# Reordering A's q and k weight columns on chip, so that most head rows skip the DRAM scratch

## The chip, the cores and the metric

One core of a Trainium2 chip runs the kernel. The time is device microseconds of one execution; the number given for a kernel is the median of several runs. TensorE (PE in the profile) multiplies, VectorE (DVE) and ScalarE (ACT) read its results out of PSUM, GpSimd (POOL) masks, and SyncE (SP) issues nearly all DMAs.

## The reference

Two attention blocks on inputs of 2048 tokens and 640 features, 32 heads of 20 features each; their outputs lie side by side. Block A is softmax attention within a sliding window of 256 tokens, block B is linear attention:

```python
def _A_ref(x, wqkv, wo):
    H = 32; Dh = D // H; W = 256
    q, k, v = qkv[0], qkv[1], qkv[2]            # (x @ wqkv) by heads
    scores = jnp.einsum("bhqd,bhkd->bhqk", q, k) * (Dh ** -0.5)
    mask = (idx[:, None] - idx[None, :] >= 0) & (idx[:, None] - idx[None, :] < W)
    p = _softmax(jnp.where(mask, scores, -1e9), axis=-1)
    o = jnp.einsum("bhqk,bhkd->bhqd", p, v)
    return o.reshape(B, S, D) @ wo

def _B_ref(x, wqkv, wo):
    phi = lambda t: jnp.where(t > 0, t + 1, jnp.exp(t)) + 1e-6
    pq, pk = phi(q), phi(k)
    kv = jnp.einsum("bhsd,bhse->bhde", pk, v);  z = jnp.einsum("bhsd->bhd", pk)
    num = jnp.einsum("bhqd,bhde->bhqe", pq, kv)
    den = jnp.einsum("bhqd,bhd->bhq", pq, z)[..., None] + 1e-6
    return (num / den).reshape(B, S, D) @ wo
```

## The kernel before

Tokens are worked in four super-blocks `s` of 512. The heads of A are taken in eight groups of four. For the scores, TensorE runs the four heads of a group side by side in four strips of 32 rows, so q and k are wanted in "pads": tiles of 128 partitions by 8 groups by 512 tokens in which head j of a group lies on partitions 32j to 32j+19. The projection gives its rows packed, 20 to a head, so before the change every q and k row takes a trip through DRAM: `a_rows(n, s)` computes five chains of five 128x512 matmuls (L208), casts each to a stage tile `st` (L198), writes it to a scratch tensor, and `bounce` queues four reads (L277) that put the rows into the pad. For s = 0 the writes are issued on ACT's queue chunk by chunk (L309), for the others as one transfer on SP (L273); the reads are issued by `drip` within later work, or by `drop` at once.

The main loop takes 90 score tiles (18 for s = 0, then 24 each). `scores` puts up to four blocks of 128 x 128 of each of four heads into `S_ps`, which fills half of PSUM and has one buffer (L587). ACT takes the exponential of all 2048 columns into `p` (L595), after a one-element copy into `p` that takes the waits for that buffer (L580), and POOL masks the edges (L609). Two tiles later `values` multiplies by v (16 matmuls of 21 columns, L631) into `O_ps`, one buffer too, and after the last tile of a head group VectorE divides by the row sums (recA L653, otokA L654). The first tile of s = 0 (form "X") takes the diagonal block of groups 0 to 3, and the tile with that of groups 4 to 7 comes at index 9.

All the other work is a generator `fill`, from which `take` draws matmuls between tiles: q, k and v of A's later super-blocks, B's projections and `b_kv`, `b_q`, `b_den`, `b_merge`, output projections. Its unit is columns of TensorE work. `credit` gives each tile an equal share of it:

```python
    take(EARLY)
    units = [u for s in range(NS) for u in tiles_of(s)]
    LAG = 2
    rate = (FILL - TAIL - LAG * NO_VALUES) / len(units)
```

`EARLY` is 25600 columns, which are the q and k rows of s = 1: they are computed ahead of tile 0, while the pads of s = 0 come back from DRAM. `TAIL` columns stay for after the last tile. Fill matmuls go to one of three PSUM banks `dense`, which VectorE (or ACT near the end) has to read before PE takes the bank again. `phi` is computed by an ACT exponential `e` (L218) and two VectorE steps (L221, L224), of which the latter are put off (`later`, `flush`). `b_den` flushes them and makes the reciprocal denominators rden (L535, L536), and `quotients` multiplies by them on VectorE (L547), with DMA transposes before and after on SP's queue.

The order of instructions on each engine is the program's order. The kernel starts with loads of x and of A's v, q and k weights on SP's queue in this order, then x of s = 1 (a DMA transpose) and B's k weights. PE runs a few dummy matmuls, transposes x, computes v of s = 0 (`a_v(0)`, casts to vA on VectorE), then q and k of s = 0, the early fill, and tile 0.

Of the kernel before, what the change touches and what calls it, by code (L numbers as in the profile page):

```python
# [9 lines left out]
P = 128  # L10
ALU = mybir.AluOpType
ACT = mybir.ActivationFunctionType
ENG = mybir.EngineType
BF16 = mybir.dt.bfloat16
# [3 lines left out]
DH = 20  # L18
HV = DH + 1
NG = H // 4  # L20
SB = 512
TPS = SB // P

EARLY = 25600
FILL = 357760
TAIL = 17920

NO_VALUES = 1024
# [26 lines left out]
def kernel(  # L55
# [10 lines left out]
    nc = tc.nc  # L66
    _, S, D = A_x.shape
    KT = D // P
# [8 lines left out]
    def pool(name, bufs, space=None):  # L77
        if space is None:
            return ctx.enter_context(tc.tile_pool(name=name, bufs=bufs))
        return ctx.enter_context(tc.tile_pool(name=name, bufs=bufs, space=space))  # L80

    wp = pool("weights", 1)
    xp = pool("x", 2)
    qp = pool("q", 2)
    kp = pool("k", 3)
    vp = pool("v", 3)
    pp = pool("p", 3)
    stp = pool("stage", 2)
    bp = pool("b", 1)
    pqp = pool("pq", 2)  # L90
    op1 = pool("o1", 2)
# [10 lines left out]
    w_sb = {}  # L102
    wo_sb = {}
    for n in "AB":
        w_sb[n] = wp.tile([P, KT, 3 * D], BF16, name=f"w{n}")
        wo_sb[n] = wp.tile([P, KT + (n == "B"), D], BF16, name=f"wo{n}")

    def load_w(n, src, i, eng, lo=0, hi=D):
        wv = src.rearrange("(kt p) n -> p kt n", p=P)
        cols = slice(i * D + lo, i * D + hi)  # L110
        eng.dma_start(out=w_sb[n][:, :, cols], in_=wv[:, :, cols])

    xsrc = {"A": A_x[0], "B": B_x[0]}

# [68 lines left out]
    def flush(before=None):  # L183

        while later and (before is None or later[0][0] <= before):
            later.pop(0)[1]()
# [3 lines left out]
    def evac(dst, src, to=None):  # L190

        if to is None and both:
            both.append(to)
            to = "AD"[len(both) % 2]
        if to == "A":
            nc.scalar.activation(out=dst, in_=src, func=ACT.Copy)
        else:
            nc.vector.tensor_copy(out=dst, in_=src)  # L198

    def bank():  # L200
        flush(begun[0] - 2)
        begun[0] += 1
        return dps.tile([P, SB], F32, name="dense")

    def chain(dst, lhs, rhs, n):

        for kt in range(KT):
            nc.tensor.matmul(  # L208
                dst, lhsT=lhs(kt), rhs=rhs(kt), start=(kt == 0), stop=(kt == KT - 1)
            )  # L210
            if kt < KT - 1:
                yield n
# [22 lines left out]
    def banks(g, n):  # L235

        for _ in range(n):
            for c in g:
                yield c
                if isinstance(c, End):  # L240
                    break
# [22 lines left out]
    xA, xB = {}, {}  # L264
    q_pad, k_pad, v_tok = {}, {}, {}

    reads = {}

    def bounce(n, s, scratch, st, dst):


        if s > 0:
            nc.sync.dma_start(out=scratch.rearrange("(c p) n -> p c n", p=P), in_=st[:])  # L273
        sv = scratch.rearrange("(g j d) n -> j d g n", j=4, d=DH)

        def read(j):
            nc.sync.dma_start(out=dst[32 * j : 32 * j + DH, :, :], in_=sv[j])  # L277

        reads[n, s] = [(read, j) for j in range(4)]

# [12 lines left out]
            fn(j)  # L293

    def a_rows(n, s):
        base = 0 if n == "q" else D
        st = stp.tile([P, KT, SB], BF16, name="st")
        scratch = tc.dram_tile([D, SB], BF16, name=f"{n}_scr{s}")
        for c in range(KT):
            ps = bank()  # L300
            yield from chain(
                ps[:],
                lambda kt: w_sb["A"][:, kt, base + c * P : base + (c + 1) * P],
                lambda kt: xA[s][:, kt, :],
                SB,
            )
            evac(st[:, c, :], ps[:])
            if s == 0:
                nc.scalar.dma_start(out=scratch[c * P : (c + 1) * P, :], in_=st[:, c, :])  # L309
            if c == KT - 1:  # L310
                pad, pl, name = (q_pad, qp, "qpad") if n == "q" else (k_pad, kp, "kpad")
                pad[s] = pl.tile([P, NG, SB], BF16, name=name)
                bounce(n, s, scratch, st, pad[s])
            yield End(SB)

    def a_qk(s, between=()):
# [5 lines left out]
    def hook(gen, n, fn):  # L322

        for i, c in enumerate(gen):
            if i == n:
                fn()
            yield c

    hh = H // 2
    by_tokens = [(tb, i) for tb in range(TPS) for i in range(2)]  # L330

    def v_proj(n, xt, dst, order=by_tokens):
        for tb, i in order:
            ps = bank()
            yield from chain(
                ps[:, 0 : hh * DH],
                lambda kt: xt[:, kt, tb * P : (tb + 1) * P],
                lambda kt: w_sb[n][:, kt, 2 * D + i * hh * DH : 2 * D + (i + 1) * hh * DH],
                hh * DH,
            )  # L340
            evac(
                dst[:, tb, i * hh : (i + 1) * hh, 0:DH],
                ps[:, 0 : hh * DH].rearrange("p (h d) -> p h d", d=DH),
            )
            yield End(hh * DH)
# [7 lines left out]
    def a_v(s):  # L353
        v_tok[s] = v_bufs[s % 3]
        order = by_tokens
        if s == 0:
            order = [(0, 0), (1, 0), (0, 1), (1, 1), (2, 0), (2, 1), (3, 0), (3, 1)]
        yield from v_proj("A", xA[s], v_tok[s], order)
# [50 lines left out]
    def b_kv(s):  # L409
        pk = pqp.tile([P, TPS, D], BF16, name="phi")  # L410

        def done(tb, ps):
            if tb is None:
                phi(pk[:, :, SB:D], ps, lambda t: t[:].rearrange("p (t n) -> p t n", n=P))
            else:
                phi(pk[:, tb, 0:SB], ps[:])

        rows = tok_rows(xB[s], w_sb["B"], D, done)
        values_of = v_proj("B", xB[s], vB)
        yield from even(rows, TPS + 1, values_of, TPS + 1)  # L420
        yield from values_of
        flush()
        for cs in (range(0, 3), range(3, KT)):
            ps = bank()
            pv = ps[:, 0 : len(cs) * NHC * HV].rearrange("p (c h e) -> p c h e", h=NHC, e=HV)
            for i, c in enumerate(cs):
                for tb in range(TPS):
                    nc.tensor.matmul(  # L428
                        pv[:, i, :, :],
                        lhsT=pk[:, tb, c * P : (c + 1) * P],  # L430
                        rhs=vB[:, tb, GH * c : GH * c + NHC, :],
                        start=(tb == 0),
                        stop=(tb == TPS - 1),
                    )
                if c != cs[-1]:
                    yield TPS * P + P
            at = slice(cs[0], cs[-1] + 1)
            acc = kv_acc[:, at, :, :]
            if s == 0:
                nc.vector.tensor_copy(out=acc, in_=pv)  # L440
            elif s < NS - 1:
                nc.vector.tensor_tensor(out=acc, in0=pv, in1=acc, op=ALU.add)
            else:
                for dst, h0, h1, e0, e1 in (
                    (zk, 0, NHC, DH, HV), (six, 0, GH, 0, DH), (two, GH, NHC, 0, DH)
                ):
                    nc.vector.tensor_tensor(
                        out=dst[:, at, :, :],
                        in0=pv[:, :, h0:h1, e0:e1],
                        in1=acc[:, :, h0:h1, e0:e1],  # L450
                        op=ALU.add,
                    )
            yield TPS * P + P
# [235 lines left out]
    def run(gen):  # L689
        for _ in gen:  # L690
            pass
# [22 lines left out]
    def load(n, s):  # L714
        if n == "A":
            xA[s] = load_x("A", s)
        else:
            xB[s] = load_x("B", s % NS)
        yield 0
# [11 lines left out]
    load_w("A", A_wqkv, 2, nc.sync, 0, hh * DH)  # L731
    load_half(1)
    load_w("A", A_wqkv, 2, nc.sync, hh * DH, D)
    for i in range(2):
        load_w("A", A_wqkv, i, nc.sync)
    run(load("A", 1))
    load_w("B", B_wqkv, 1, nc.sync)
    dummies = warm_up((28, 3))
# [1 line left out]
    transposes(0)  # L740
    next(dummies)
    run(hook(a_v(0), 2 * KT - 1, lambda: transposes(1)))

    def late_load(n, w):

# [17 lines left out]
    def k_reads(s, gen):  # L763
        return drip(gen, ("k", s), 8, 5)

    early = seq(a_qk(3), k_reads(3, a_v(3)))
    q = [b_q(s) for s in range(NS)]
# [7 lines left out]
        spread(b_kv(2), [("B", 3)], 15),  # L775
        spread(a_qk(2), [("B", NS)], 10),
        k_reads(2, a_v(2)),
        banks(early, KT),
        b_kv(3),
        spread(even(q[0], KT, early, KT), [("B", NS + 1)], 1),  # L780
        spread(
            seq(banks(q[1], 2), b_den(0), even(q[1], KT - 2, early, 3)), [("B", NS + 2)], 10
# [15 lines left out]
    def take(cols):  # L798
        done = 0.0
        while done < cols:  # L800
            try:
                done += next(fill)
            except StopIteration:
                break
        return done

    take(EARLY)
    units = [u for s in range(NS) for u in tiles_of(s)]
    LAG = 2
    pend = deque()  # L810
    rate = (FILL - TAIL - LAG * NO_VALUES) / len(units)
    credit = 0.0
    for i, (okey, first, last, parts) in enumerate(units):
        p = scores(okey[0], parts)
# [46 lines left out]
```

## Time and profile before

| what | value |
|---|---|
| median of 3 runs | 278.11 us (277.8 to 278.4) |
| span of the profiled execution, first to last instruction | 276.4 us |
| granted TensorE clock, mean | 1.000 |
| PE busy | 268.4 us, 97% |
| ACT busy | 202.1 us, 73% |
| VectorE busy | 172.8 us, 63% |
| POOL busy | 163.7 us, 59% |
| first matmul of A's q rows | 12.51 us |
| first exponential of a score tile | 35.18 us |
| last exponential of a score tile | 254.98 us |

The profile is of one execution. Its own time outside the span is not recorded; the span is 1.7 us shorter than the median of the runs. A busy time is the union of an engine's instructions; matmuls overlap, so a mean duration of a matmul is longer than the distance between two starts, and the distances tell what PE needs. "idle before, releaser" tells how long an engine had waited and for what.

### The profile page before, as it was taken

The numbers are of one execution on the slowest core, as the hardware profiler recorded it, in microseconds if no ns is written. First come the engines' busy times: TensorE is split into PE (matmuls) and PEld (weight loads), VectorE is DVE, ScalarE is ACT, GpSimd is POOL, SyncE is SP. The second block draws the span as 40 slices with busy tenths as digits, with TensorE's granted clock in tenths as the row PEclk, the third lists the DMA queues.
The fourth block names the chain that finished last, engine by engine and source line by source line (L and its number), as shares of the span: only waits on it lengthen the run. The fifth ranks groups of instructions, "written<-read, shape, count | busy, mean of one in ns | idle before, by whom it ended". The sixth has DMA issues, their size and how long they took to land.

```text
span 276.4 us, 8281 instructions
## 1 busy us (share of the span) xinstructions
PE 268.4 (97%) x3507; PEld 154.5 (56%) x3507; DVE 172.8 (63%) x337; ACT 202.1 (73%) x231; POOL 163.7 (59%) x204
## 2 busy tenths in 40 slices
PE   8999999999999999999999999999999999999993
PEld 7644465665665764564566445565644564555651
DVE  0666665566757755555566564799687668779420
ACT  2100079989988977877998999986899889987331
POOL 5000056675766667666667797676687768788510
PEclk9999999999999999999999999999999999999999
DMA  6986899899744951762216533769979757446384
GB/s 196 326 240 190 165 276 182 145 141 221 185 56 82 178 77 61 145 165 41 97 27 99 90 91 80 187 91 122 152 175 146 109 130 161 93 94 123 130 235 127
DMA packets 82094, 38.88 MB, mean 141 GB/s; under 512 B 64137, under 2 KB 81161, under 8 KB 82057
## 3 DMA queue, kind: packets, MB, share of 16 engines
q1 hardware_dynamic: 79609, 32.46, 59.9%
q0 software_dynamic: 1008, 4.59, 5.0%
q10 hardware_dynamic: 1440, 1.31, 1.4%
q8 instruction: 27, 0.44, 0.7%
q14 instruction: 10, 0.08, 0.1%
HBM read 12.45 MB, written 10.49 MB: 83 GB/s over the span
## 4 chain that ended last, share of the span: by engine, by line
PE 79%; DVE 6%; DMA 5%; ACT 4%; issue 2%; SPq 2%; ACTq 0%
PE dense L208 50%; PE O_ps L631 14%; PE S_ps L587 10%; ACT p L595 3%; PE dense L428 2%; DMA kpad<-k_scr 2%; DMA oT<-otokA 2%; SPq L665 2%; DVE vB L547 2%; DMA k_scr<-st 1%; PE dense L152 1%; DVE osb L198 1%; PE dense L477 1%; DVE otokA L654 1%; PE dense L133 1%
## 5 line engine op out<-in xcount | busy, mean ns | idle before, releaser
L609 POOL TENSOR_SCALAR_AFFINE_SELECT p<-p 128x512 bf16<-128x512 bf16 (+1 forms) x180 | 151.6, 842 | 95.8 <-ACT p L595 89.1
L595 ACT ACTIVATE p<-S_ps 128x2048 bf16<-128x2048 f32 x90 | 168.7, 1875 | 36.8 <-PE S_ps L587 36.2
L631 PEld LDWEIGHTS <-p 128*128 128x128 bf16 x1440 | 42.3, 96 | 19.0 <-issue 17.3
L631 PE MATMUL O_ps<-vA,p 128*128 128x21 bf16 x1440 | 50.7, 173 | 0.3 <-DVE otokA L654 0.3
L208 PE MATMUL dense<-wB,xB 128*128 128x320 bf16 (+2 forms) x320 | 48.4, 298 | 0.0
L208 PE MATMUL dense<-xA,wA 128*128 128x512 bf16 x200 | 46.5, 379 | 0.0
L198 DVE CAST st<-dense 128x512 bf16<-128x512 f32 x40 | 27.6, 690 | 21.5 <-PE dense L208 20.8
L587 PE MATMUL S_ps<-qpad,kpad 20*128 20x256 bf16 (+2 forms) x736 | 36.1, 270 | 1.1 <-DMA kpad<-k_scr 0.3
L208 PEld LDWEIGHTS <-xA 128*128 128x128 bf16 x320 | 27.0, 98 | 15.4 <-issue 0.9
L208 PEld LDWEIGHTS <-xB 128*128 128x128 bf16 x320 | 26.0, 97 | 11.9
L587 PEld LDWEIGHTS <-kpad 20*128 20x128 bf16 x736 | 12.5, 92 | 32.0 <-issue 30.1
L198 DVE CAST osb<-dense 128x512 bf16<-128x512 f32 x31 | 21.2, 686 | 13.8 <-PE dense L208 13.7
L208 PEld LDWEIGHTS <-wA 128*128 128x128 bf16 x200 | 18.6, 97 | 20.0
L224 DVE SCALAR_TENSOR_TENSOR phi<-dense,e 128x512 bf16<-128x512 f32 x40 | 27.7, 691 | 1.4
L580 ACT ACTIVATE p<-ident 1x1 bf16<-1x1 bf16 x90 | 16.9, 188 | 15.5 <-DMA qpad<-q_scr 15.5
L208 PE MATMUL dense<-woA,oT 128*128 128x512 bf16 (+1 forms) x160 | 24.7, 299 | 2.0 <-DMA oT<-otokA 2.0
L208 PE MATMUL dense<-xB,wB 128*128 128x512 bf16 x100 | 26.6, 378 | 0.0
L208 PE MATMUL dense<-wA,xA 128*128 128x320 bf16 x160 | 25.4, 303 | 0.3 <-DVE phi L224 0.2
L221 DVE TENSOR_SCALAR e<-e 128x512 bf16<-128x512 bf16 x40 | 15.6, 390 | 15.2 <-ACT e L218 14.6
L208 PE MATMUL dense<-wB,xA 128*128 128x512 bf16 (+1 forms) x160 | 25.0, 299 | 0.0
L218 ACT ACTIVATE e<-dense 128x512 bf16<-128x512 f32 x40 | 23.7, 593 | 0.9 <-PE dense L208 0.2
L198 DVE CAST vA<-dense 128x320 bf16<-128x320 f32 x32 | 15.7, 489 | 11.0 <-PE dense L208 10.8
(44 smaller groups left out, 148.6 us busy)
## 6 DMA issues: line engine op xcount, KB each, us to landing
out_dram<-osb POOLq DMA_DIRECT2D x7, 640.0 KB, 4.2
qpad<-q_scr SPq DMA_DIRECT2D x16, 160.0 KB
kpad<-k_scr SPq DMA_DIRECT2D x16, 160.0 KB
wB<-in_B_wqkv_dram SPq DMA_DIRECT2D x3, 800.0 KB
q_scr<-st SPq DMA_DIRECT2D x3, 640.0 KB
k_scr<-st SPq DMA_DIRECT2D x3, 640.0 KB
wA<-in_A_wqkv_dram SPq DMA_DIRECT2D x2, 800.0 KB
wA<-in_A_wqkv_dram SPq DMA_DIRECT2D x2, 400.0 KB
```

The costliest lines, as they stand in the source:

```text
L198: nc.vector.tensor_copy(out=dst, in_=src)
L208: nc.tensor.matmul(dst, lhsT=lhs(kt), rhs=rhs(kt), start=(kt == 0), stop=(kt == KT - 1))
L218: nc.scalar.activation(out=view(e), in_=src, func=ACT.Exp)
L221: nc.vector.tensor_scalar(out=e[:], in0=e[:], scalar1=1e-6, scalar2=1.0 + 1e-6, op0=ALU.add, op1=ALU.min)
L224: nc.vector.scalar_tensor_tensor(out=dst, in0=src, scalar=0.0, in1=view(e), op0=ALU.max, op1=ALU.add)
L428: nc.tensor.matmul(pv[:, i, :, :], lhsT=pk[:, tb, c * P : (c + 1) * P], rhs=vB[:, tb, GH * c : GH * c + NHC, :], start=(tb == 0), stop=(tb ...
L547: nc.vector.tensor_tensor(out=vh, in0=vh, in1=rden_of[s][:, tb, :, :].to_broadcast([P, H, DH]), op=ALU.mult)
L580: nc.scalar.activation(out=p_all[0:1, 4 * SB : 4 * SB + 1], in_=ident[0:1, 0:1], func=ACT.Copy)
L587: nc.tensor.matmul(S_ps[:, j, blk * P : blk * P + n], lhsT=kt[32 * j : 32 * j + DH, g, ko : ko + P], rhs=q_pad[s][32 * j : 32 * j + DH, g, ...
L595: nc.scalar.activation(out=p, in_=S_ps[:], func=ACT.Exp, scale=scale)
L609: nc.gpsimd.affine_select(out=v, in_=v, pattern=[[0, 4], [0, b1 - b0], [sgn, P]], compare_op=ALU.is_ge, fill=0.0, base=0 if kind == "D" el ...
L631: nc.tensor.matmul(O_ps[:, slot, j, :], lhsT=p[:, j, b * P : (b + 1) * P], rhs=v_tok[kb // TPS][:, kb % TPS, 4 * gg + j, :], start=(first ...
```

## The change

The columns of A's q and k weights are put into another order on chip, so that each chain of `a_rows` gives 128 rows that are laid out like a pad. Chunk c (of five) holds, for each of four strips j, the 20 features of head j of group c, and in the remaining 12 rows of the strip a part of the features of groups 5 to 7. So groups 0 to 4 go straight from PSUM to the pad by the cast, and only the extra rows (60 a strip) go through scratch: `moves` writes them from the pad to DRAM in four transfers and queues four reads that bring them back as groups 5 to 7.

The raw weights are loaded into buffers of the pads (`load_raw`), and `regroup` copies them into `wqk` after `a_v(0)`: for q the heads in one copy on VectorE and seven pieces on ACT, for k the heads on ACT and seven pieces on POOL. `EARLY` goes: nothing lies between the k rows of s = 0 and tile 0, and its columns are added to `FILL`, so that every tile's share rises. `b_kv(3)` is put ahead of the q rows of s = 3.

```diff
-EARLY = 25600
-FILL = 357760
+FILL = 383360
...
+    EXTRA = 32 - DH
+    wqk = wp.tile([P, 2, KT, D], BF16, name="wqk")
+    pieces = []
+    for c in range(KT):
+        m = EXTRA * c
+        while m < EXTRA * (c + 1):
+            n = min(EXTRA * (c + 1) - m, DH - m % DH)
+            pieces.append((c, DH + m - EXTRA * c, KT + m // DH, m % DH, n))
+            m += n
+
+    def load_raw(i):
+        pl, name = ((qp, "qpad"), (kp, "kpad"))[i]
+        t = pl.tile([P, NG, SB], BF16, name=name)
+        raw = t.rearrange("p g q -> p (g q)")[:, 0 : KT * D].rearrange("p (k n) -> p k n", n=D)
+        wv = A_wqkv.rearrange("(kt p) n -> p kt n", p=P)
+        nc.sync.dma_start(out=raw, in_=wv[:, :, i * D : (i + 1) * D])
+        return raw
+
+    def regroup(i, src, heads, extras):
+        dst = wqk[:, i, :, :]
+        w = KT * 4 * DH
+        heads(
+            dst.rearrange("p k (h e) -> p k h e", e=32)[:, :, :, 0:DH],
+            src[:, :, 0:w].rearrange("p k (h d) -> p k h d", d=DH),
+        )
+        for c, row, g, d, n in pieces:
+            extras(
+                dst[:, :, c * P : (c + 1) * P].rearrange("p k (j e) -> p k j e", e=32)[
+                    :, :, :, row : row + n
+                ],
+                src[:, :, 4 * DH * g : 4 * DH * (g + 1)].rearrange("p k (j d) -> p k j d", d=DH)[
+                    :, :, :, d : d + n
+                ],
+            )
...
-    def bounce(n, s, scratch, st, dst):
-        if s > 0:
-            nc.sync.dma_start(out=scratch.rearrange("(c p) n -> p c n", p=P), in_=st[:])
-        sv = scratch.rearrange("(g j d) n -> j d g n", j=4, d=DH)
+    def moves(n, s, pad):
+        scratch = tc.dram_tile([4, KT * EXTRA, SB], BF16, name=f"{n}_scr{s}")
+        for j in range(4):
+            nc.sync.dma_start(
+                out=scratch[j].rearrange("(c e) q -> e c q", e=EXTRA),
+                in_=pad[32 * j + DH : 32 * (j + 1), 0:KT, :],
+            )
         def read(j):
-            nc.sync.dma_start(out=dst[32 * j : 32 * j + DH, :, :], in_=sv[j])
+            nc.sync.dma_start(
+                out=pad[32 * j : 32 * j + DH, KT:NG, :],
+                in_=scratch[j].rearrange("(g d) q -> d g q", d=DH),
+            )
...
     def a_rows(n, s):
...
-                lambda kt: w_sb["A"][:, kt, base + c * P : base + (c + 1) * P],
+                lambda kt: wqk[:, i, kt, c * P : (c + 1) * P],
                 lambda kt: xA[s][:, kt, :],
                 SB,
             )
-            evac(st[:, c, :], ps[:])
-            if s == 0:
-                nc.scalar.dma_start(out=scratch[c * P : (c + 1) * P, :], in_=st[:, c, :])
+            evac(pad[:, c, :], ps[:])
             if c == KT - 1:
-                bounce(n, s, scratch, st, pad[s])
+                moves(n, s, pad)
...
-    for i in range(2):
-        load_w("A", A_wqkv, i, nc.sync)
+    raw = [load_raw(i) for i in range(2)]
...
     run(hook(a_v(0), 2 * KT - 1, lambda: transposes(1)))
+    regroup(0, raw[0], dve_copy, act_copy)
+    regroup(1, raw[1], act_copy, pool_copy)
...
         k_reads(2, a_v(2)),
+        b_kv(3),
         banks(early, KT),
-        b_kv(3),
...
-    take(EARLY)
```

More of the change, by code (lines that the diff above doesn't have):

```diff
@@ L87 @@
     pp = pool("p", 3)
-    stp = pool("stage", 2)
     bp = pool("b", 1)
@@ L104 @@
     for n in "AB":
-        w_sb[n] = wp.tile([P, KT, 3 * D], BF16, name=f"w{n}")
+        w_sb[n] = wp.tile([P, KT, (1 if n == "A" else 3) * D], BF16, name=f"w{n}")
         wo_sb[n] = wp.tile([P, KT + (n == "B"), D], BF16, name=f"wo{n}")
@@ L110, in load_w @@
         cols = slice(i * D + lo, i * D + hi)
-        eng.dma_start(out=w_sb[n][:, :, cols], in_=wv[:, :, cols])
+        dst = w_sb[n][:, :, lo:hi] if n == "A" else w_sb[n][:, :, cols]
+        eng.dma_start(out=dst, in_=wv[:, :, cols])
     xsrc = {"A": A_x[0], "B": B_x[0]}
@@ new lines, in act_copy, with dve_copy, pool_copy @@
+    def act_copy(dst, src):
+        nc.scalar.activation(out=dst, in_=src, func=ACT.Copy)
+    def dve_copy(dst, src):
+        nc.vector.tensor_copy(out=dst, in_=src)
+    def pool_copy(dst, src):
+        nc.gpsimd.tensor_copy(out=dst, in_=src)
+    reads = {}
+    def moves(n, s, pad):
[5 more added lines that the diff above has]
+            )
@@ L295, in a_rows @@
     def a_rows(n, s):
-        base = 0 if n == "q" else D
-        st = stp.tile([P, KT, SB], BF16, name="st")
-        scratch = tc.dram_tile([D, SB], BF16, name=f"{n}_scr{s}")
+        i = 0 if n == "q" else 1
+        pads, pl, name = (q_pad, qp, "qpad") if n == "q" else (k_pad, kp, "kpad")
+        pad = pads[s] = pl.tile([P, NG, SB], BF16, name=name)
         for c in range(KT):
@@ L306, in a_rows @@
             )
-            evac(st[:, c, :], ps[:])
-            if s == 0:
-                nc.scalar.dma_start(out=scratch[c * P : (c + 1) * P, :], in_=st[:, c, :])
+            evac(pad[:, c, :], ps[:])
             if c == KT - 1:
-                pad, pl, name = (q_pad, qp, "qpad") if n == "q" else (k_pad, kp, "kpad")
-                pad[s] = pl.tile([P, NG, SB], BF16, name=name)
-                bounce(n, s, scratch, st, pad[s])
+                moves(n, s, pad)
             yield End(SB)
@@ L332, in v_proj @@
     def v_proj(n, xt, dst, order=by_tokens):
+        v0 = 0 if n == "A" else 2 * D
         for tb, i in order:
@@ L337, in v_proj @@
                 lambda kt: xt[:, kt, tb * P : (tb + 1) * P],
-                lambda kt: w_sb[n][:, kt, 2 * D + i * hh * DH : 2 * D + (i + 1) * hh * DH],
+                lambda kt: w_sb[n][:, kt, v0 + i * hh * DH : v0 + (i + 1) * hh * DH],
                 hh * DH,
```

## The prediction

> **What bounds the kernel now.** I read the page's busy times and slices first, then the windows of the start and of the tiles, then the timeline of the start, of two tiles and of one busy place, and the groups for durations.
>
> ```profile
> PE 268.4 (97%) x3507; PEld 154.5 (56%) x3507; DVE 172.8 (63%) x337; ACT 202.1 (73%) x231; POOL 163.7 (59%) x204
> ACT  2100079989988977877998999986899889987331
> ```
>
> TensorE (PE) is busy 97% of the span, ScalarE (ACT) only from the sixth slice on. The windows (columns: length, then busy time of PE, weight load, VectorE, ACT, POOL) say the same by stage:
>
> ```profile
> 12.50:34.20 21.70, 21.70 (x105) 9.72 (x102) 13.65 (x21) 0.20 (x1) 0.00 (x0) 1.00 0.79 202
> 34.20:255.00 220.80, 219.25 (x3158) 126.27 (x3157) 148.70 (x296) 192.52 (x219) 155.06 (x187) 1.00 0.66 126
> ```
>
> From 12.5 to 34.2 us PE runs 100 projection matmuls, half of them (`take(EARLY)`) only to cover the scratch trip of tile 0, while ACT idles. That looks like 10 us to be won, if PE is not needed later. So the question is whether the tiles have room for those 50 matmuls. The timeline of the start and of two tiles:
>
> ```profile
> 12.51 21.75 PE L208 MATMUL dense<-xA,wA 128*128 128x512 bf16 x100
> 12.71 0.49 DVE L198 CAST vA<-dense 128x320 bf16<-128x320 f32 x1 [0.18 <-PE dense L208]
> ...
> 34.75 0.39 PE L587 MATMUL S_ps<-qpad,kpad 20*128 20x128 bf16 x13 [0.33 <-DMA kpad<-k_scr]
> 35.18 1.88 ACT L595 ACTIVATE p<-S_ps 128x2048 bf16<-128x2048 f32 x1 [10.38 <-PE S_ps L587]
> ...
> 99.49 1.88 ACT L595 ACTIVATE p<-S_ps 128x2048 bf16<-128x2048 f32 x1 [0.54 <-PE S_ps L587]
> 99.79 1.89 PE L208 MATMUL dense<-xA,wA 128*128 128x512 bf16 x8
> 101.61 0.40 PE L587 MATMUL S_ps<-qpad,kpad 20*128 20x384 bf16 x8
> 101.94 0.57 PE L631 MATMUL O_ps<-vA,p 128*128 128x21 bf16 x16
> 102.06 1.88 ACT L595 ACTIVATE p<-S_ps 128x2048 bf16<-128x2048 f32 x1 [0.61 <-PE S_ps L587]
> 102.36 1.67 PE L208 MATMUL dense<-xA,wA 128*128 128x512 bf16 x7
> 103.99 0.40 PE L587 MATMUL S_ps<-qpad,kpad 20*128 20x256 bf16 x8
> 104.43 1.88 ACT L595 ACTIVATE p<-S_ps 128x2048 bf16<-128x2048 f32 x1 [0.41 <-PE S_ps L587]
> ```
>
> A tile on PE: scores to values 101.94 - 101.61 = 0.33 us, 16 values products 102.36 - 101.94 = 0.42, each 512-column fill matmul 21.75/100 = 0.216, and some 0.095 to change from fill to scores. With 8 fill matmuls that is 2.57 (99.49 to 102.06), with 7 it is 2.36. On ACT: exponential 1.88, scores 0.40 because S_ps has one buffer, two hand-overs of 0.05: 2.37 (102.06 to 104.43). So PE and ACT are level at 7 fill matmuls a tile; every one beyond costs its full 0.216. The 89 steps between the first and last exponential take 254.98 - 35.18 = 219.8. Adding up PE's need tile by tile in program order gives 216.5; raising tiles under 2.37 to that floor, 217.8. The 2.0 left are waits for VectorE (DVE), mostly around `b_den` and the quotients.
>
> **The change, part by part.** The sum is made on the profiled execution, span 276.4; the median of the runs is 278.11, 1.7 more, and I carry that over.
>
> *Start.* `a_v(0)` still ends on PE at 12.5. Then PE waits for the first regrouping copy: `dve_copy` of q's heads (128 x 2000 bf16, SBUF to SBUF) stands on DVE behind the last vA cast, which ends at 12.71 + 0.49 = 13.20. Its price has no row. The nearest is the only bf16 copy-like step inside SBUF:
>
> ```profile
> L221 DVE TENSOR_SCALAR e<-e 128x512 bf16<-128x512 bf16 x40 | 15.6, 390 | 15.2 <-ACT e L218 14.6
> ```
>
> Less a fixed part of 0.155 (casts of 320 and 512 elements take 0.489 and 0.690, so 1.05 ns an element and 0.155 fixed), that is 0.46 ns an element, or 1.07 us for 2000. Above stands the cast rate, 2.25; below, L221's quickest instance in the timeline, 0.28, or 0.25 ns and 0.65 us. I take 1.1, the mean of the nearest row, since POOL copies at the same time. The Trainium skill, VectorE: DVE Perf Modes (What auto-detection actually checks; The perf-mode tier table), lists a 2048-element bf16 copy in SBUF at 693 ns, if the outer sizes of both patterns are even or equal; by that the sum would be 0.4 lower, and no run here shows it yet.
>
> So q starts at 13.2 + 1.1 = 14.3 instead of 12.5: +1.8 of PE idle. The rest of the regrouping is hidden. ACT's seven q pieces (80 to 240 elements; from the rows for 1 and 512 elements, 0.19 and 0.60, about 0.3 each, 2.2 in all) need the raw weights, which had landed by 12.5 since PE used them then: the first is done by 12.9, the last by 14.8, and the fifth chain wants it only at 14.3 + 4.3. k's heads on ACT (0.19 + 2000 x 0.8 ns = 1.8) and seven POOL pieces (0.3 fixed plus 0.8 ns an element by L609, about 0.45 each) have until 19.7. Without that cover, each us would count fully.
>
> The k chains end at 14.3 + 50 x 0.216 = 25.1 and tile 0's scores follow at once, since it reads groups 0 to 3 alone: no wait for the bounce (0.56 before, 34.19 to 34.75). First exponential at 25.1 + 0.43 = 25.5 against 35.18: 9.7 earlier.
>
> *Tiles.* The same 50 matmuls, 10.8 us of PE, now lie among the tiles, on average 7.9 instead of 7.3 of 512 columns each. By program order of the changed kernel PE's need is 227.2, with the ACT floor 227.4: only four tiles are still under the floor, so 9.5 us more than 217.8, and the slack won back is the difference, 1.3.
>
> *Waits for DVE.* The 2.0 of before stay, and the shifted order adds some. Here is `b_den(0)` before, in the timeline (DVE and the PE instruction that waits):
>
> ```profile
> 173.03 0.37 DVE L221 TENSOR_SCALAR e<-e 128x512 bf16<-128x512 bf16 x1 [0.79 <-ACT e L218]
> 173.43 0.69 DVE L224 SCALAR_TENSOR_TENSOR phi<-dense,e 128x512 bf16<-128x512 f32 x1
> 174.04 0.28 DVE L535 TENSOR_SCALAR rden<-dense 128x128 f32<-128x128 f32 x1
> 174.17 0.84 PE L208 MATMUL dense<-wA,xA 128*128 128x320 bf16 x5 [0.23 <-DVE phi L224]
> 174.35 0.95 DVE L536 RECIPROCAL rden<-rden 128x128 f32<-128x128 f32 x1
> ```
>
> There, a head group's recA/otokA pair had left DVE just before. In the changed order the pair stands behind two e, two phi, rden and its reciprocal: 2 x (0.39 + 0.69) + 0.28 + 0.95 + 0.25 + 0.49 = 4.1 us of DVE. It can begin 2.8 after a tile's scores (0.45 + 1.88 + e 0.49) and so ends after 6.9; O_ps has one buffer, and PE wants it for the next group 2 x 2.57 + 0.33 = 5.5 after those scores: 1.4 of wait. Around the quotients and `b_den(1)` the queue otokA, quotient, rden, reciprocal, wB (0.49 + 0.95 + 0.28 + 0.95 + 0.48 = 3.2) stands against a tile of 2.6, and merge chains fill the three dense banks quickly: I put 0.9. New waits 2.3, from 0 (DVE frees the buffers in time) to 4 (both places and one more).
>
> *Hidden.* Casts go to the pads rather than to `st` at the same 0.69. A bounce moves 240 KB out and 240 back instead of 640; SP issues 8 transfers each instead of 5, 18 more over s = 1 to 3 at 0.4 to 0.5. SP has the room except from 166 to 200 us, where k(3)'s writes add 1.2 ahead of the transposes that the quotients read (before, DVE waited 0.4 for one). Swapping `b_kv(3)` and `banks(early)` changes no work. Tile 9 reads the groups from scratch over 20 us after they are issued.
>
> *Sum.* Last exponential at 25.5 + 227.4 + 2.0 + 2.3 = 257.2 against 254.98: +2.2. The end (three values steps, four transposes, `a_out_last`) has the same order and keeps its 21.4. Span 278.6, time 280.3.
>
> **The rivals.**
> *The tiles absorb the fill* (faster): if ACT were the limit everywhere, tiles stayed at 2.47 and everything came 9.7 earlier, 268.4. The tile with 8 matmuls at 2.57 speaks against it. A smaller form is real: the O_ps and bank waits go instead of growing (only 1.0 left of all waits) and the copy takes 0.65. Then the last exponential is at 25.1 + 227.4 + 1.0 = 253.5, -1.5, time 276.6. It decides where waits in the loop fall below 2.1. For it: DVE is only 63% busy. Together 0.12.
> *An exact swap*: waits stay at 2.0, 25.5 + 229.4 = 254.9, time 278.0. Chance 0.15.
> *Late loads* (slower still): B's first x and value weights are issued on SP after tile 0's bounce and q(1)'s writes, about 34.6, and the x transpose holds SP 6.1 (as at 30.29 before), so the weights go out at 41 and, by the 5 us or so of the wB load at 13.01, land near 46; the first product with them stands near 51. If the writes' landings hold SP 5 us longer it counts one to one: with a cast-rate copy of 2.25 or larger DVE waits, +4 to +6, 282 to 284. Chance 0.18.
> *The clock falls in the gap*: the granted clock is 1.00 in both windows above, and no gap of 1.8 us in mid-kernel is there to show what one does. The slow clock is seen at the start alone: the 28 warm-up matmuls of 128 columns from 1.06 on take 3.17 us, 0.113 each, and later ones 0.055, and it lasts until about 7 us. As long a slow stretch after the gap, 6 us at half speed, would cost 3.0, 283.3; chance 0.03. The Trainium skill, TensorE: Matmul & The Clock Gate (Part 1), sets the clock back after an idle window of about 3.4 us, which this gap does not fill.
>
> **How the numbers follow.** The forecast, 280.3, has 0.52. About 0.2% (0.56 us) is what a measurement can tell from no change. Faster 0.12; same, most of the swap, 0.14; slower 0.74. The range 277.9 to 283.0 takes in the swap, the forecast with both copy bounds and waits up to 4, and leaves out the faster cases and the worst late loads.
>
> **What would show it.** In the changed profile: q's first matmul at 13.9 to 15.5 with DVE wqk as releaser; first exponential near 25.5; most tiles at 2.57, the 89 steps 230 to 233 in sum; a wait of PE for otokA of over 1 us near 177. Wrong would be steps that sum below 229, or a PE wait for a load of B near 48.

## The result and the profile after

The changed kernel takes 281.33 us (median of 4 runs, 280.25 to 282.25), the kernel before in the same session 278.15: a ratio of 1.0108, 95% interval 1.0076 to 1.014. By the medians it is 3.2 us slower; the forecast was 280.3 in a range of 277.9 to 283.0. The profiled execution took 282.25 with a span of 280.5, the longest of the four (the others: 278.5, 279.5 and 279.7), so what is read from it lies about 0.9 us above the median. Ratios below leave out runs far above their kernel's quickest, medians don't.

The busy times and the slices of ScalarE in the changed kernel's page:

```profile
PE 267.0 (95%) x3507; PEld 152.9 (54%) x3507; DVE 175.1 (62%) x338; ACT 207.4 (74%) x239; POOL 167.0 (60%) x211
ACT  2512777998998977788987898887789779788432
```

ScalarE now works from the fourth slice on instead of the sixth, and PE's share has fallen from 97 to 95%. The windows of the start and of the tiles (length, then busy time of PE, weight load, VectorE, ACT, POOL; the granted clock third from the end):

```profile
12.50:26.03 13.53, 11.76 (x71) 5.25 (x69) 8.44 (x13) 1.97 (x4) 1.96 (x7) 1.00 0.51 119
26.03:260.21 234.18, 228.78 (x3196) 129.72 (x3195) 156.68 (x306) 194.31 (x219) 156.78 (x187) 1.00 0.55 103
```

In the tiles PE is idle for 234.18 - 228.78 = 5.4 us; before it was 1.6 of 220.8, of which 0.33 was the wait for the bounce ahead of tile 0. The start and the end of the matter in the timeline:

```profile
13.36 1.18 DVE L310 COPY wqk<-qpad 128x2000 bf16<-128x2000 bf16 x1
...
14.69 10.95 PE L207 MATMUL dense<-xA,wqk 128*128 128x512 bf16 x50 [1.77 <-DVE wqk L310]
...
25.57 0.40 PE L637 MATMUL S_ps<-qpad,kpad 20*128 20x128 bf16 x16
...
26.03 1.88 ACT L645 ACTIVATE p<-S_ps 128x2048 bf16<-128x2048 f32 x1 [11.18 <-PE S_ps L637]
```

So the first exponential comes 9.15 us earlier (26.03 instead of 35.18), the 89 steps to the last one take 14.38 more (234.18 instead of 219.80), and from there to the end it is 20.34 instead of 21.45. Together +4.1, the 276.4 to 280.5 of the spans. About 1.1 of this belongs to the execution rather than to the change: two later profiles with the same loop (other engines, longer gap) both have 233.06 for the steps, and the one wait that they lack, 1.07 at 237.08, is shown further down. What PE waited for, in the table of waits (total, times, longest), in the changed kernel and then before:

```profile
PE O_ps L681 <- DVE otokA L704: 2.1, 2, 1.1
PE dense L207 <- DVE wqk L310: 1.8, 1, 1.8
PE dense L207 <- DVE phi L223: 1.7, 3, 0.7
PE dense L207 <- DMA oT<-otokA: 1.2, 2, 0.9
```

```profile
PE dense L208 <- DMA oT<-otokA: 2.0, 2, 1.6
PE O_ps L631 <- DVE otokA L654: 0.3, 1, 0.3
PE dense L208 <- DVE phi L224: 0.2, 1, 0.2
```

So the waits for O_ps and phi in the loop are nearly all new. How a wait for phi arises is seen here:

```profile
97.72 1.84 POOL L659 TENSOR_SCALAR_AFFINE_SELECT p<-p 128x512 bf16<-128x512 bf16 x2 [0.63 <-ACT p L645]
...
98.48 1.23 DVE L220 TENSOR_SCALAR e<-e 128x512 bf16<-128x512 bf16 x1 [1.22 <-ACT e L217]
...
99.82 0.69 DVE L223 SCALAR_TENSOR_TENSOR phi<-dense,e 128x512 bf16<-128x512 f32 x1
...
100.56 0.57 PE L207 MATMUL dense<-wB,xB 128*128 128x320 bf16 x3 [0.54 <-DVE phi L223]
```

VectorE's e step, 0.28 us at its quickest, takes 1.23 and ends at 99.71, 0.15 after GpSimd's masks end (97.72 + 1.84 = 99.56). Then phi is late, the bank of `dense` is late, and PE stands for 0.54.

### The profile page after: what moved, and what is told of

It reads as the page before. It is cut to its first block, busy times and chain, and to the rows that moved or that the text cites. A ratio compares the mean times of both kernels' runs of the same rounds, so it can differ in the third digit from the quotient of the medians.

```text
span 280.5 us, 8302 instructions
## 1 busy us (share of the span) xinstructions
PE 267.0 (95%) x3507; PEld 152.9 (54%) x3507; DVE 175.1 (62%) x338; ACT 207.4 (74%) x239; POOL 167.0 (60%) x211
## 4 chain that ended last, share of the span: by engine, by line
PE 81%; DVE 7%; DMA 5%; ACT 2%; SPq 2%; issue 1%; POOL 0%; DVEq 0%
PE dense L207 54%; PE O_ps L681 14%; PE S_ps L637 9%; DMA wA<-in_A_wqkv_dram 2%; PE dense L478 2%; SPq L715 2%; DMA oT<-otokA 2%; ACT p L645 1%; DVE e L220 1%; DVE phi L223 1%; DVE otokA L704 1%; DMA tok<-phi 1%; DVE tok L597 1%; PE dense L527 1%; ACT e L217 1%
## 5 line engine op out<-in xcount | busy, mean ns | idle before, releaser
L207 PE MATMUL dense<-xA,wqk 128*128 128x512 bf16 x200 | 47.4, 378 | 1.8 <-DVE wqk L310 1.8
L220 DVE TENSOR_SCALAR e<-e 128x512 bf16<-128x512 bf16 x40 | 18.0, 451 | 21.4 <-ACT e L217 21.3
L207 PEld LDWEIGHTS <-wqk 128*128 128x128 bf16 x200 | 18.0, 97 | 21.0 <-issue 2.3
L637 PEld LDWEIGHTS <-kpad 20*128 20x128 bf16 x736 | 11.1, 92 | 29.9 <-issue 28.9
L207 PE MATMUL dense<-xB,wB 128*128 128x512 bf16 x100 | 25.6, 378 | 0.5 <-DVE phi L223 0.5
L197 DVE CAST qpad<-dense 128x512 bf16<-128x512 f32 x20 | 13.8, 692 | 13.5 <-PE dense L207 13.4
L197 DVE CAST vB<-dense 128x320 bf16<-128x320 f32 x32 | 15.4, 488 | 8.2 <-PE dense L207 8.0
L197 DVE CAST kpad<-dense 128x512 bf16<-128x512 f32 x20 | 13.7, 690 | 10.8 <-PE dense L207 10.8
```

The costliest lines, as they stand in the source:

```text
L207: nc.tensor.matmul(dst, lhsT=lhs(kt), rhs=rhs(kt), start=(kt == 0), stop=(kt == KT - 1))
L220: nc.vector.tensor_scalar(out=e[:], in0=e[:], scalar1=1e-6, scalar2=1.0 + 1e-6, op0=ALU.add, op1=ALU.min)
L637: nc.tensor.matmul(S_ps[:, j, blk * P : blk * P + n], lhsT=kt[32 * j : 32 * j + DH, g, ko : ko + P], rhs=q_pad[s][32 * j : 32 * j + DH, g, ...
```

## The experiments

Theory A is that of the prediction: an exchange of 10.8 us of fill between the start, where PE is the only busy engine, and tiles in which PE is the limit as well; what is lost on top is the gap ahead of q and new waits for VectorE. The rivals: that the fill's place itself is wrong (tiles too full), that the copy is slow only since it contends with GpSimd, and that a gap of PE lowers its clock.

### The early fill put back

```diff
-FILL = 383360
+EARLY = 25600
+FILL = 357760
...
+    take(EARLY)
     units = [u for s in range(NS) for u in tiles_of(s)]
```

> The changed kernel with the early fill put back: the 25600 columns of q and k of s = 1 are drawn ahead of tile 0 again (EARLY 25600, FILL 357760); regrouping and direct rows stay. Theory A (the tiles are bound by TensorE, and the moved matmuls cost their own time there plus new waits for VectorE): first exponential near 36.9 (26.03 + 50 x 0.217), steps back to about 220 to 222 in sum, so 1.5 to 2.5 us faster than the changed kernel, near 279.3, and 1 to 1.5 slower than before, which is the 1.8 us of waiting for the regrouping less the 0.56 of waiting for the bounce. Theory B (the new transfers and the regrouping cost the time): it stays at 281 or goes above, since tile 0 comes 10.9 later again. Theory C (the early start does gain, and something else loses more): slower than the changed kernel by several us.

Measured: 280.76 us (279.48 to 282.79), ratio 1.007 (1.0041 to 1.0099). In its profiled execution, the quickest of its runs at a span of 277.8, the first exponential is at 36.38, the 89 steps take 220.72 and the tail 20.67: the loop is nearly that of the kernel before (219.80), and 10.35 us are lost at the start for 13.46 won in the tiles (12.3 against the 233.06 of the other two profiles). By the ratios the new place of the fill costs some 0.4% (1.0108 against 1.007; the intervals overlap), by the medians 0.6 us, less than the 1.5 to 2.5 that theory A expected, so it is close to an exchange. The other 0.7% are there without it: the gap of 1.78 ahead of q stands in this kernel too.

### Other engines for the regrouping

```diff
-    regroup(0, raw[0], dve_copy, act_copy)
-    regroup(1, raw[1], act_copy, pool_copy)
+    regroup(0, raw[0], act_copy, pool_copy)
+    regroup(1, raw[1], dve_copy, act_copy)
```

> The changed kernel with the regrouping on other engines: q's heads on ACT and its pieces on POOL, both free from 10.7 us on when the raw q weights land; k's heads on VectorE and its pieces on ACT. Theory A: q's first matmul moves from 14.69 to about 12.9, and all that follows with it, 1.2 to 1.8 us faster than the changed kernel. Theory B (the gap is covered by slack later): no change. Also open: the price of the copy of 2000 elements on VectorE. If its 1.18 us held a wait for POOL's copies beside it, it takes about 0.68 here, where POOL is done by 13; if not, 1.18 again.

Measured: 279.62 us (278.69 to 279.89), ratio 1.0028 (1.001 to 1.0045). The timeline of its start:

```profile
10.23 1.87 ACT L307 ACTIVATE wqk<-qpad 128x2000 bf16<-128x2000 bf16 x1 [1.74 <-DMA qpad<-in_A_wqkv_dram]
...
12.27 1.46 PE L207 MATMUL dense<-xA,wqk 128*128 128x512 bf16 x5
...
12.88 1.19 DVE L310 COPY wqk<-kpad 128x2000 bf16<-128x2000 bf16 x1
```

ScalarE is free from 10.2, so its copy of 1.87 lies beside the last products of v, and q starts with no gap. The first exponential is at 23.61, 2.4 earlier than in the changed kernel (1.9 earlier than the 25.5 that two other profiles with that kernel's start have), and the steps take 233.06. The gap's price is therefore about 0.8% (1.0108 to 1.0028; 1.7 us by the medians), the larger part of the loss. The same copy by VectorE takes 1.19 here, after GpSimd's last q piece ended at 12.22: it was not GpSimd that made it 1.18, and that rival is out.

### Another share for each tile

```diff
-FILL = 383360
+FILL = 378860
```

> The changed kernel with one constant changed, FILL 378860 for 383360: every tile's share of fill is 50 columns (1.2%) less, 4500 columns more are left after the last tile, and the group ends fall elsewhere against b_den and the quotients. All work is the same. Theory A (2 to 5 us of the tiles' steps are waits for VectorE that depend on what stands next to what): the wait of PE for otokA near 180 (1.0) goes or moves, the steps sum to 228 to 231 instead of 234.2, and the time is 277 to 279.5. Theory B (the steps are TensorE work alone): the steps fall by the 50 x 90 columns moved, 1.9 us, and the tail takes them back: 281, no change.

Measured: 276.65 us (275.78 to 280.0), ratio 0.9914 (0.9882 to 0.9947), faster than both kernels and just below the 277 to 279.5 expected; 25.55 to the first exponential, steps 227.97, tail 20.96. 4500 columns less in the tiles are worth 4500 / 512 x 0.216 = 1.9 us, which the tail takes over; it grows by only 0.6, since the 1.2 of waits for oT are gone there. The steps fell by 6.2, so about 4.3 us are waits that went (3.2 against the 233.06 of the other two profiles). All the waits of PE over 0.2 us, in this kernel's table:

```profile
PE dense L207 <- DVE wqk L310: 1.8, 1, 1.8
PE dense L151 <- DVE osb L147: 1.1, 1, 1.1
PE dense L207 <- DMA wA<-in_A_wqkv_dram: 0.4, 1, 0.4
PE dense L527 <- DVE vA L197: 0.3, 2, 0.2
```

Neither O_ps nor phi nor oT is left. The e steps are not quicker for it, at a mean of 452 ns as in the changed kernel (451): late e steps now stand where PE has other work. So at this share it is the place of the delays, not their amount, that set the time.

### The kernel before at another share

```diff
-FILL = 357760
+FILL = 353260
```

> The kernel before with a planned fill among the tiles of 353260 instead of 357760, the same step down as the one that made the changed kernel 1.7 % faster. Theory (a different share moves the meetings of VectorE and PE; before has only about 1 us of waits for VectorE in its loop, so it has little to win and as much to lose): 276.5 to 279.5, within 1 us of the kernel before either way. Rival (a smaller share is better in itself, since less work stands among the tiles and the rest falls into the end, where PE waits anyway): 273 to 275, as much of a gain as in the changed kernel.

Measured: 279.09 us (278.47 to 280.96), ratio 1.0023 (1.0001 to 1.0044); first exponential 35.56, steps 220.58. A smaller share is no gain in itself: the kernel before had about 1 us of such waits to lose, and here others come (0.6 for a mask, 0.4 for wB).

### No masks, in both kernels

In the changed kernel and in the one before, GpSimd's edge masks on p are left out:

```diff
-        for kind, b0, b1 in sorted(runs, key=lambda r: r[2] - r[1]):
+        for kind, b0, b1 in []:
```

> The changed kernel without POOL's edge masks on the exponentials (this part of the computation is left out). VectorE's first step on e (L220) took 0.28 where POOL was idle when it began and ended 0.15 after POOL's mask where one ran, up to 1.23. Theory A (VectorE waits for POOL in these steps, and PE for VectorE): all 40 take 0.28, the waits of PE for phi and otokA shrink, steps sum to 229 to 231, time 277 to 279. Theory B (the long ones come from something else): durations and time as in the changed kernel, but for the 3.9 us in which the weight load waited for a mask.

> The kernel before without GpSimd's edge masks on p (left out: the zeroing of products outside the window). It pairs with the changed kernel without masks, whose span fell from 280.5 to 276.6 us and whose time fell to 1.001 of the time before. Theory (the e step of VectorE ends late beside a mask, and the changed order of the work meets more masks at places where TensorE stands behind e): all 40 e steps take 0.28 to 0.30 here too, but PE waits only 4.1 us in all in the kernel before, 0.5 of them for VectorE in the loop, so the 89 steps gain little: 218.3 to 219.8 instead of 219.8, span 275.0 to 276.4, time 276.7 to 278.2. Rival (masks slow both kernels alike, and the exchange of the start for the tiles has nothing to do with them): the span falls by the 3.9 us of the changed kernel, to about 272.5.

Measured: changed without masks 278.71 us, ratio 1.0013 (0.9981 to 1.0044), steps 230.71 instead of 234.18; before without masks 276.95, ratio 0.9942 (0.9919 to 0.9964), steps 219.24 instead of 219.80. The group of the e step with masks in the changed kernel, then in the two without (count, busy us, mean ns):

```profile
L220 DVE TENSOR_SCALAR e<-e 128x512 bf16<-128x512 bf16 x40 | 18.0, 451 | 21.4 <-ACT e L217 21.3
```

```profile
L220 DVE TENSOR_SCALAR e<-e 128x512 bf16<-128x512 bf16 x40 | 11.6, 290 | 24.6 <-ACT e L217 24.6
```

```profile
L221 DVE TENSOR_SCALAR e<-e 128x512 bf16<-128x512 bf16 x40 | 12.0, 300 | 16.8 <-ACT e L218 16.3
```

With no mask running, every e step of the changed kernel takes 0.28 to 0.30 us. In the kernel before 39 of 40 do, and the one that doesn't, 0.66 us at 153.62, stands beside another select of GpSimd (on wB, from 153.21). That masks delay e is shown by this. Of the 14.38 us by which the steps grew, the masks make 3.47 - 0.56 = 2.9 in the profiled executions, or 1.8 when the 233.06 of the other two profiles is taken for the changed kernel. Not all of it need be the e step: without masks PE's weight loads don't wait for them either (3.9 us in seven waits in the changed kernel, of which PE itself stood 0.2). By the times the share is smaller and uncertain: the two kernels lie 1.08% apart with masks and 0.71% without, a difference of some 1 us with intervals as wide. PE's wait for otokA remains in the changed kernel without masks, with 0.8; it belongs to the order.

### Engines and share together

Three kernels join the engines of the second experiment with other shares. The diff of the first; the second has `FILL = 378860` and no early fill, the third `EARLY = 2560` and `FILL = 369440`:

```diff
-FILL = 383360
+EARLY = 7680
+FILL = 366820
...
+    regroup(0, raw[0], act_copy, pool_copy)
+    regroup(1, raw[1], dve_copy, act_copy)
...
+    take(EARLY)
```

> The changed kernel with the first regrouping on ScalarE and GpSimd and the second on VectorE and ScalarE, 7680 columns of fill (15 matmuls of 512) ahead of tile 0 and a planned fill of 366820 among the tiles instead of 383360. Theory (the cost is the gap of 1.8 us ahead of q, which the engine swap takes away, and the waits of PE for VectorE, which go with another share per tile; matmuls moved between the start and the tiles otherwise count alike): first exponential at 23.6 + 15 x 0.216 = 26.8, the 89 steps 222 to 226, last exponential 249 to 253, tail 20.3 to 21.0, span 270 to 274, time 271.5 to 275.5. Rival (the waits come back with any share that was not searched for, as in the changed kernel): steps 226 to 229, last exponential 253 to 256, span 273.5 to 277, time 275 to 278.5.

> The changed kernel with both edits that were run alone: the first regrouping on ScalarE and GpSimd and the second on VectorE and ScalarE (alone: span 277.0 instead of 280.5, q's first matmul at 12.3), and a planned fill of 378860 (alone: span 274.5, no PE wait for O_ps). Theory (the gap ahead of q and the waits in the loop are separate terms): first exponential at 23.6, steps 228 to 229, tail 20.3 to 21, span 272 to 273.5, time 274 to 275. Rival (the 2 us at the start are taken back by the loop, because ScalarE is then on its floor or because the waits come back with the earlier start): steps 230 or more, span 274 to 276, time 275.5 to 277.5.

> The changed kernel with the other engines for the regrouping, 2560 columns of fill (5 matmuls of 512) ahead of tile 0 and a planned fill of 369440 among the tiles. Theory (start and waits are separate terms, and the clock stays whole where no wait of PE reaches 2 us): first exponential at 24.4 + 5 x 0.216 = 25.5, steps 224 to 227, span 271 to 274, all runs within 1.5 us of each other, time 272.5 to 275.5, faster than before by 1 to 2 %. Rival (at other shares VectorE's meetings with GpSimd and with late transposes make a PE wait of 2 us again, and a halved clock behind it): span 275 to 278 in a part of the runs, median 276 to 278.

| kernel | median (runs) | ratio | first exponential, steps, tail |
|---|---|---|---|
| 7680 ahead, 366820 | 277.31 (274.12 to 279.89) | 0.9924 (0.9891 to 0.9957) | 26.65, 226.07, 23.00 |
| none ahead, 378860 | 276.42 (274.11 to 278.73) | 0.9888 (0.9839 to 0.9937) | 24.41, 227.94, 20.96 |
| 2560 ahead, 369440 | 275.81 (275.1 to 277.82) | 0.9919 (0.9893 to 0.9944) | 25.49, 225.08, 23.54 |

All three beat both kernels, by about 1% against the one before. Among themselves and against the share alone (0.9914) they can't be told apart. The engine swap, worth 0.8% beside the old share, shows only 0.3% beside the new one, within the intervals: it is not shown that the two terms add up. The start of the second came 0.8 later than the 23.6 expected, with a wait of 0.7 for x.

The second and the third missed their expectations of 274 to 275 and 272.5 to 275.5: of the six runs of the second three lie at 274.1 to 275.1 and three at 277.7 to 278.7, and the third's median is 0.3 above its range. The first missed its expectation of 271.5 to 275.5 by more, and its profile shows a part of the reason. It held a wait that the profiles of the others did not:

```profile
230.57 0.82 DVE L598 TENSOR_TENSOR tok<-tok,rden 128x640 bf16<-128x640 bf16 x1 [3.28 <-DMA tok<-phi]
...
231.21 1.89 POOL L660 TENSOR_SCALAR_AFFINE_SELECT p<-p 128x512 bf16<-128x512 bf16 x2
231.31 0.77 DVE L221 TENSOR_SCALAR e<-e 128x512 bf16<-128x512 bf16 x1
...
232.86 0.59 PE L208 MATMUL dense<-wB,xA 128*128 128x512 bf16 x2 [2.04 <-DVE phi L224]
...
235.32 1.92 PE L208 MATMUL dense<-xB,wB 128*128 128x512 bf16 x4
```

A quotient on VectorE waited 3.28 for a DMA transpose, with e and phi queued behind it; e then met a mask, and PE stood still for 2.04. Then four matmuls of 512 columns take 1.92, where four at 227.63 took 1.03. One window of a microsecond within that stretch (the granted clock is third from the end):

```profile
235.00:236.00 1.00, 1.00 (x4) 0.35 (x3) 0.97 (x4) 0.79 (x2) 0.23 (x1) 0.50 0.35 68
```

By the windows from 234 to 238 (clocks of 0.60, 0.50, 0.50 and 0.69) it is 0.50 for about 0.8 + 1 + 1 + 0.6 = 3.4 us. In 8 of this kernel's 12 runs the mean clock is 0.987 to 0.994, at spans of 275.5 to 278.2; its quickest runs, at 0.999 and 1.000, have 272.4 and 273.2, inside the expectation. Two more runs at 0.999 and 1.000 have 275.1 and 275.4, so the clock is not the whole of the miss. One stretch like this lowers the mean clock by 0.5 x 3.4 / 276 = 0.006, and the second kernel shows as much in two of six runs (0.992 and 0.994), the third in one of nine (0.993); their profiled executions were at 1.000. That is the prediction's clock rival, in another place than it was looked for.

### A longer gap ahead of q

```diff
+    dve_copy(
+        wqk[:, 0, :, :].rearrange("p k (h e) -> p k h e", e=32)[:, :, :, 0:DH],
+        raw[0][:, :, 0 : KT * 4 * DH].rearrange("p k (h d) -> p k h d", d=DH),
+    )
     regroup(0, raw[0], dve_copy, act_copy)
```

> The changed kernel with VectorE's copy of q's heads issued twice, which makes the gap of PE ahead of q's first matmul one copy (1.18 us) longer: 2.95 instead of 1.77 us. It settles the prediction's rival of the clock. Theory A (a gap ahead of q costs its own length and no more): q's first matmul at 15.9, its matmuls 0.216 each, first exponential at 27.2, and the span about 1.2 longer, 281.7, time 282.5. Theory B (a gap of over about 2 us also halves the clock, as the wait of 2.04 us at 230.8 in the run with another share and other engines did, where 3 to 4 us at 0.50 followed): part of the q chains runs at 0.43 to 0.48 a matmul, the granted clock shows a stretch at 0.5 behind 15.9, the first exponential comes at 28.5 to 30.5, span 283 to 285.

Measured: 284.24 us (282.67 to 284.77), ratio 1.0209 (1.0179 to 1.024), span 282.0. Its q and k chains in the timeline, and one window:

```profile
15.66 12.64 PE L207 MATMUL dense<-xA,wqk 128*128 128x512 bf16 x50 [3.01 <-DVE wqk L310]
```

```profile
17.00:18.00 1.00, 1.00 (x4) 0.35 (x3) 0.63 (x1) 0.00 (x0) 0.00 (x0) 0.50 0.37 128
```

Against the changed kernel the gap is 3.01 - 1.77 = 1.24 longer, but the 50 chain matmuls take 28.23 - 15.66 = 12.57 from the first to tile 0's scores instead of 10.88: 1.69 more. By the windows from 16 to 21 (clocks of 0.90, 0.50, 0.50, 0.50 and 0.90) that is half clock for about 3.4 us, from 16.8 to 20.2. The first exponential, 28.68, lies in theory B's range. Three of its four runs have a mean clock of 0.994 and the fourth 1.000, so a gap of 3 us lowers the clock often and not always. The changed kernel's 1.77 did not, by its clock of 0.999 to 1.000 in all four runs.

## Why the prediction was right, and where not

**The direction and the mechanism hold.** Tiles with eight fill matmuls take 2.57 as forecast (25 of the 89 steps lie at 2.56 and 2.57), and more than the early start won, 9.15, was paid back in the loop, 14.38.

**The start** (forecast 25.5, measured 26.03). The copy took 1.18, where 1.1 was taken, and began at 13.36 instead of 13.2; the hand-over to PE of 14.69 - 13.36 - 1.18 = 0.15 was not in the sum. The rest is 0.1. Two other profiles with the same start have 25.55 and 25.52 (the smaller share and the one without masks), so 0.5 is also what one execution can differ from another; in the changed kernel's profile PE waited 0.5 for x in the first transposes. All of ACT's and GpSimd's pieces stayed hidden. The other copy price, of the Trainium skill, VectorE: DVE Perf Modes (The perf-mode tier table), 693 ns for 2048 bf16 elements in SBUF, was not reached: 1.18 here, 1.19 beside ScalarE alone, and 2.42 for the two copies of the longer gap, of which the last 0.9 ran after the copies of ScalarE and GpSimd had ended.

**The waits for VectorE** are the term that was mis-sized: 2.0 of before plus 2.3 new were taken, the profiled execution has 234.2 - 227.4 = 6.8, so 4.8 new instead of 2.3, above even the upper end of 4; the steps also lie above the 230 to 233 that were named as the sign. In the other two profiles of this loop, with 233.06, it is 3.7. Of the 6.8 the trace shows 5.4 as idle time of PE. The wait at `b_den(0)` is there, 1.02 where 1.4 was worked out, 3 us behind the place named:

```profile
178.35 0.95 DVE L586 RECIPROCAL rden<-rden 128x128 f32<-128x128 f32 x1
...
179.45 0.49 DVE L704 TENSOR_TENSOR otokA<-O_ps,recA 128x320 bf16<-128x320 f32 x1
...
180.09 0.55 PE L681 MATMUL O_ps<-vA,p 128*128 128x21 bf16 x16 [1.02 <-DVE otokA L704]
```

A second like it fell in the stretch for which 0.9 had been put. The first line shows it. The second, from the table of waits of the kernel with the longer gap, shows that PE waited for O_ps only once there, as in the kernel with the other engines:

```profile
237.08 0.55 PE L681 MATMUL O_ps<-vA,p 128*128 128x21 bf16 x16 [1.07 <-DVE otokA L704]
```

```profile
PE O_ps L681 <- DVE otokA L704: 1.0, 1, 1.0
```

So the 0.9, which was to cover the banks of `dense` as well, was too small: PE's waits for a bank behind a late phi alone are 1.7 in three waits. Two of the three come behind an e of about 1.2, and without masks 0.4 of the 1.7 is left. A price that helped to hide them is the 0.39 in "2 x (0.39 + 0.69)": it was taken as the price of an e, though it is a mean of two kinds. A step is said here to have met a mask when one was running as it began and ran on for over 0.03 us. Of the 40 e steps of the kernel before, 8 met no mask and took 0.28 in the mean, and the 32 that met one took 0.42 in the mean, 1.2 at most. In the changed order 29 met one and took 0.51 in the mean, five of them over 1.1. The trace of before showed this, had the instances been looked at one by one beside GpSimd.

The Trainium skill states the cause that fits: SBUF — State Buffer (Who interferes with whom) says that VectorE's fast two-port modes and GpSimd share one pair of ports, held by one of them for a whole instruction while the other blocks. The trace agrees: in the changed kernel every e step of over 0.3 us ends 0.14 to 0.15 after the end of the mask it met, and the six that began up to 0.04 ahead of a mask's start took 0.28 to 0.30. Of two that began 0.01 to 0.02 behind one, one took 0.28 and the other 1.23.

**The end** was forecast as unchanged and is 1.1 shorter, mostly since the two waits for oT fell from 2.0 to 1.2.

**Together**: +0.5 at the start, +2.5 in the steps, -1.1 at the end make the span 280.5 instead of 278.6. The median is only 1.0 above the forecast, since the profiled run was the longest of four. That it came so near is in part luck: the end, for which no change was forecast, took back 1.1 of the 3.0 that start and steps had too little.

**The rivals.** The late loads did not come: no wait of PE for a load of B is in the table of waits. "The tiles absorb the fill" is refuted for this order by the loop; yet its "smaller form", that the waits go instead of growing, is what a step of 1.2% in the share brings (0.9914). The prediction treated the waits as a matter of the change; they are one of where in the order the tiles cut the fill. The clock rival did not decide here. Half speed was right for it, the length was not: the longer gap lost 1.7 us in a stretch of 3.4, where 3.0 had been put for one of 6.

**Open:** what makes the runs of the changed kernel spread over 2.0 us (before, 0.6), of which the wait at 237.08, seen in one of three profiles, may be a part; why the copy stays at 1.18 (the condition that the prediction named with the 693 ns, outer sizes both even or equal, may not be met: the source is 5 blocks of 400 elements, while the destination is 100 rows of 20, all 32 apart; no run tests it); and which length of a gap decides the clock.

## What to carry to other kernels

Moving cover work from a stage where the limiting engine would idle into one where it is the limit is an exchange, so cost what comes with it: here a copy of 1.2 us on the one engine that was still busy with the stage before was about 0.8 of the 1.1% lost at this share, and the engine that was free took the copy without a gap. A mean duration in a group can hide two prices; look for instances of several times the shortest and at what another engine does just then. After a change of order, vary the share of work per tile by a per cent or two before judging it, since waits between in-order engines depend on which work meets which, and run the old order so too.

## What the runs showed of the hardware

VectorE's bf16 step within SBUF (0.28 us alone) doesn't slow down beside a GpSimd select, it stands until the select's end, up to 1.23 us.

PE's clock halved behind waits of 2.04 and 3.01 us: each was followed by about 3.4 us at 0.50, beginning 1.1 to 1.3 us after work was resumed. The 1.77 us was not followed by one. In the 3.4 us that ended where the clock fell (13.4 to 16.8 and 230.8 to 234.2) PE had stood for 2.3 and 2.0 us; that the idle share of such a stretch decides is not shown. The Trainium skill, TensorE: Matmul & The Clock Gate (Part 1), gives an idle window of about 3.4 us for this, free-running. Both gaps are shorter than that, so the measurement differs from it on the length of the gap; the slow stretch has the length of one such window, and that one of the four runs of the kernel with the longer gap kept its clock fits a window that doesn't start with the kernel.

A regrouping copy of 128 x 2000 bf16 elements in rows of 20 took 1.18 us on VectorE and 1.87 on ScalarE.
